# A gated mix of a spectral filter and a Mish MLP: exchange 1 in eight full-width writes and eight half-width reads, a reordered start and a moved end

## The chip, the core and the metric

The kernel runs on one core of one Trainium2 chip. The metric is device microseconds for one execution of the program. A profiled execution also has a span: the time from its first to its last instruction, which is a little shorter than the time. Times inside the span are given in us from its start. The engines are TensorE (PE; its weight loads are PEld), VectorE (DVE), ScalarE (ACT), GpSimd (POOL) and SyncE (SP). SP, ACT and POOL each issue transfers into a queue of their own; the 16 DMA engines serve all queues.

## The reference

Input `x` is 2048 rows of 512 in bfloat16. Two branches are computed and mixed row by row:

```
g = sigmoid(sum(x * gate_w))                       # one number per row
a = irfft2( rfft2(x) * (w_r + i w_i) )             # 2-D FFT over rows and columns, filter, back
h = x @ w1 + b1 ;  b = (h * tanh(softplus(h))) @ w2    # 512 -> 1792 -> 512, Mish
out = g * a + (1 - g) * b
```

Both branches use the same `x` (`A_x`); the second input of that shape (`B_x`) is not read.

## The kernel before, in words

All of the arithmetic that counts is matmul. The MLP is cut into 4 chunks of 512 rows. `mm1` (line 855) makes one of 14 column groups of a chunk from four matmuls of 128x512; ACT applies Mish (line 862). `mm2` (line 879) makes a tile of 128 output rows from 14 matmuls. The FFT is written as small matmuls against tables of cosines: `tr` transposes `x` (534), `a1` transforms along columns (572), `s1` (603) and `s2` (744) are the two factors of the transform along rows, the filter is multiplied in on DVE (`wm`) and combined on POOL (`wz`), `s2i` (775), `s1i` (804) and `a1i` (816) go back. `s2c` (699) is a small side calculation on the same input as `s2`. `s1` uses 64 rows of the array at a time, `s2` and `s2c` squares of 64x32, `s2i` 32x64; the other matmuls use all 128 rows.

Between `s1` and `s2`, and between `s2i` and `s1i`, the data must change partitions. That is done through DRAM: **exchange 1** writes `Y1` (in `Ybuf`) to the scratch tensor `scr1` (lines 613-615) and reads it back into `In2` (in `Abuf`, lines 682-685); **exchange 2** does the same with `scr2` (786, 791). Exchange 1 needs all of its eight groups of rows written before the first read. A group is two `s1` results: DVE or ACT copies them from PSUM to `Ybuf` (`e2`, line 610), and two transfers per group, one for each `rho` (even and odd partitions), write 64 partitions each. Four reads of 128 partitions follow. `s2` of step 0 needs read 0 alone; `s2c` needs all four.

The order of the work on each engine is not written by hand. Every operation is a task with an assumed duration and a priority, and a list scheduler (`_Graph.schedule`, 203-317) walks through them with assumed times at which loads land (`LAND`), a time up to which PE is counted at half speed (`COLD`), and a small random part in the priorities (`SEED`, `NOISE`). It fixes each engine's order when the program is built; at run time engines wait on semaphores, and each engine executes strictly in that order. Loads of `x`, `w1` and tables are issued at the start by SP and ACT in turns, `w2` and the filter weights `WT` by POOL.

At the start PE runs 16 matmuls on a zeroed tile that nobody reads (`warm`, 482-485); DVE sets that tile to zero first (477). At the end SP, having issued its last store, waits for every load that it has not yet waited for (940-943), and then for all stores (944). The last output tile is computed in two halves of 256 columns (`part`, 870-895), each with its own matmuls, its own DVE operation (891) and its own store.

Of the kernel before, what the change touches and what calls it, by code (L numbers as in the profile page):

```python
# [13 lines left out]
NT = 16  # L14
# [12 lines left out]
def _build_consts():  # L27
# [30 lines left out]
    def ee(g, rho, u):  # L58
        return 16 * g + 8 * rho + u

    a = np.arange(64)
    e_q = np.array([ee(g, rho, u) for u in range(8) for g in range(4) for rho in range(2)])
# [39 lines left out]


def _kind(name):
    return name.split("_")[0] if "_" in name else name.rstrip("0123456789")
# [47 lines left out]
class _Graph:  # L153
# [49 lines left out]
    def schedule(self):  # L203
# [13 lines left out]
        rng = np.random.RandomState(SEED)  # L217
        prio = {id(t): t.prio + OFFS.get(_kind(t.name), 0.0) + NOISE * rng.uniform(-1, 1) for t in tasks}
# [8 lines left out]
        while left:  # L227
# [92 lines left out]
NBF = 14  # L320
# [5 lines left out]
SEED = 1294  # L326
NOISE = 0.02
OFFS = {}
# [3 lines left out]
NWARM = 16  # L332
COLD = 4.5
LAND = dict(ld_x0=2.8, ld_x1=3.0, ld_x2=3.5, ld_x3=3.7, ld_w1_0_0=5.6, ld_w1_0_1=5.2,
            ld_fd=5.8, ld_b1=4.7, ld_w1_2_0=7.6, ld_w1_2_1=7.2, ld_x4=9.1, ld_x6=8.4,
            ld_w1_4_0=10.6, ld_w1_4_1=9.9, ld_x8=11.9, ld_m10=13.2, ld_x12=14.5, ld_w1_8_0=15.2,
            ld_w1_8_1=15.9, ld_m11=17.3, ld_w1_12_0=17.7, ld_w1_12_1=18.1, ld_gw=18.4, ld_sm=20.1,
            ld_gd=20.3)
# [3 lines left out]
def _build(nc, A_x, A_w_r, A_w_i, B_x, B_w1, B_b1, B_w2, gate_w, out):  # L342
# [3 lines left out]
    scr1 = nc.dram_tensor("scr1", (2, 32, 64, 256), BF)  # L346
# [4 lines left out]
    with es:  # L351
# [64 lines left out]
        scr1_w = scr1.rearrange("rho b q k -> rho q b k")  # L416
        scr1_r = scr1.rearrange("rho b (ri j) k -> (rho b ri) (j k)", ri=2)
# [52 lines left out]
        t_id = G.add("ident", "pool", 0.3, lambda e: e.affine_select(out=ident[:, :], in_=ident[:, :], pattern=[[1, 2], [2, 64]],  # L470
# [6 lines left out]
        G.add("wz", "dve", 0.3, lambda e: e.memset(act[:, 2, 0, :], 0.0), writes=["warm"])  # L477
        G.add("ebz", "pool", 0.2, lambda e: e.memset(b1f[:, 0:1], 0.0), writes=["b1z"])
        t_tab = G.add("table", "act", 1.3, lambda e: e.activation(b1f[:, 1:2], b1f[:, 0:1], AF.Mish), reads=["b1z"], writes=["b1t"], prio=0.0)

        pw = _Ps([6])
        tw = []
        for i in range(NWARM):
            tw.append(pe(f"warm{i}", mm(256), lambda e: e.matmul(ps[:, pw.bank, 0:256], act[:, 2, 0, 0:128], act[:, 2, 0, 0:256], start=True, stop=True),  # L484
                         reads=["warm"], alloc=pw if i == 0 else None, frees=[pw], prio=0.0, deps=tw[-1:]))
# [15 lines left out]
        ld_w1(0, 2, both)  # L501
        dma("ld_fd", FDs[:].rearrange("p r k -> p (r k)"), d_FD[:], writes=["FD"], nbytes=131072)
        dma("ld_b1", braw[:, :], B_b1.rearrange("(ft p) -> ft p", p=128), writes=["braw"], nbytes=3584, queue="pool", deps=[t_id])
# [23 lines left out]
        for t0, w in ((0, 1), (1, 1), (2, 2), (4, 2), (6, 2), (8, 2), (10, 2), (12, 2), (14, 2)):  # L527
            pt = _Ps(SPEC[::-1])
            def f_tr(e, t0=t0, w=w, pt=pt):
                ins = None  # L530
                for i in range(w):
                    for c in range(4):
                        o, d0 = (c * w + i) * 128, 256 * (c // 2) + c % 2
                        ins = e.transpose(psb[:, pt.bank, o:o + 128], xo[:, t0 + i, d0:d0 + 255:2], ident[:, :])  # L534
                return ins

            pe(f"tr{t0}", 4 * w * mm(128), f_tr, reads=[("x", t0 + i) for i in range(w)] + ["ident"], writes=[("ptr", t0)], alloc=pt)
            evict(f"evx{t0}", 512 * w, lambda t0=t0, w=w: xT[:, :, 128 * t0:128 * (t0 + w)],
                  lambda pt=pt, w=w: psb[:, pt.bank, 0:512 * w].rearrange("p (c j) -> p c j", c=4), rate=2.0,
                  reads=[("ptr", t0)], writes=[("xT", t0 + i) for i in range(w)], frees=[pt], engs=("dve",))  # L540
            if t0 == 2:
                pb = _Ps(SPEC[::-1])
                pe("tr_small", 0.1, lambda e, pb=pb: e.transpose(psb[:, pb.bank, 0:14].rearrange("p (a b) -> p a b", b=2), braw[0:14, :],
                                                                    ident[0:14, :].rearrange("p (b a) -> p a b", b=2)[:, 0:7, :]),
                   reads=["braw", "ident"], writes=["ptb"], alloc=pb)
                G.add("ev_small", "dve", 0.2, lambda e, pb=pb: e.tensor_copy(out=b1f[:, :], in_=psb[:, pb.bank, 0:14]),
                      reads=["ptb", "b1t"], writes=["b1f"], frees=[pb])
# [3 lines left out]
        for t in range(NT):  # L551
# [39 lines left out]
            if t % 4 == 3:  # L591
# [17 lines left out]
                for tp, p1 in zip((t - 3, t - 1), p1s):  # L609
                    evict(f"e2_{tp}", 1024, lambda tp=tp: Y1[:, 2 * tp:2 * tp + 4, :].rearrange("p (i b) k -> p i b k", b=2),  # L610
                          lambda p1=p1: ps[:, p1.sl, :].rearrange("p b (i k) -> p i b k", i=2),
                          reads=[("p1", tp)], writes=[("Y1", tp)], frees=[p1], prio=PR["sp"] + E2P, engs=("act",) if tp % 4 else ("dve",))
                    for rho in range(2):
                        dma(f"r1w{tp}{'ab'[rho]}", scr1_w[rho][:, 2 * tp:2 * tp + 4, :], Y1[rho::2, 2 * tp:2 * tp + 4, :], reads=[("Y1", tp)],
                            writes=[("scr1", tp, rho)], nbytes=64 * 4 * 512, prio=PR["sp"] + 1.0, tail=0.5, bw=300e3)
        S1R = [("scr1", i, rho) for i in range(0, NT, 2) for rho in range(2)]
# [64 lines left out]

        for v in range(4):
            dma(f"r1r{v}", In2[:, 2 * v:2 * v + 2].rearrange("p u g k -> p (u g k)"),
                scr1_r[:, 2048 * v:2048 * v + 2048], reads=S1R, writes=[("In2", rho, 2 * v + i) for i in range(2) for rho in range(2)], deps=s1_tasks,
                nbytes=128 * 4096, prio=PR["sp"] + 1.0)
        r1rs = [dma_ for dma_ in G.tasks[-4:]]
# [154 lines left out]
        def store(t):  # L841
            dma(f"out{t}", ov[:, t - 1:t + 1, :], xo[:, t - 1:t + 1, :], reads=[("o", t - 1), ("o", t)],
                nbytes=128 * 2048, is_out=True, prio=PR["fin"], tail=0.6)

        mm2s = {}
        for c in range(NCH):
            hb = c % 3
            G.cur_prio = PR["mm1"] - c
            for ft in range(NFT):
                pd = _Ps(DENSE[c])  # L850

                def f_mm1(e, c=c, ft=ft, pd=pd):
                    ins = None
                    for i in range(4):
# [10 lines left out]
                      reads=[("pm", c, ft), "b1f"], writes=[("act", hb, ft)] + (["warm"] if hb == 2 and ft == 0 else []), frees=[pd], prio=PR["mish"])  # L865
            G.cur_prio = PR["mm2"] - c
            for tl in range(4):
                t = 4 * c + tl

                for part in range(2):  # L870
                    if part == 0 or t == NT - 1:
                        pd = _Ps(DENSE2[c])
                    cs_ = slice(256 * part, 256 * part + 256) if t == NT - 1 else slice(0, 512)
# [9 lines left out]
                    tk = pe(f"mm2_{t}_{part}", 7 * mm(512), f_mm2,  # L883
# [4 lines left out]
                    if t < NBF or (t < NT - 1 and part == 0):  # L888
                        continue
                    G.add(f"fin_{t}_{part}", "dve", dve_dur(256 if t == NT - 1 else 512, True),  # L890
# [4 lines left out]
                        nbytes=65536 * (1 if t == NT - 1 else 2), is_out=True, prio=PR["fin"], tail=0.6)  # L895
# [22 lines left out]
        def run_engine(ename, eobj):  # L918
            seen = {}
            for t in order[ename]:  # L920
                need = {}
# [18 lines left out]
            if ename == "sp":  # L940
                for t in G.tasks:
                    if t.isdma and t.sem is not out_sem and seen.get(t.sem.num, 0) < t.semval:
                        eobj.wait_ge(t.sem, t.semval)
# [67 lines left out]
```

## Time and profile before

| | |
|---|---|
| median of 3 runs | 133.02 us (132.97 to 135.15) |
| the profiled execution | 132.8 us, its span 131.1 us |
| PE busy | 124.9 us, 95% of the span |
| DVE, ACT, POOL busy | 89.3, 72.2, 58.3 us |
| mean granted TensorE clock | 1.00 |
| moved by DMA | 21.09 MB, mean 161 GB/s |
| first `mm1` starts / last matmul ends | 7.29 / 128.15 us |

How to read it: PE is busy almost throughout, so what matters is when its useful work starts, whether a wait opens a hole in it, and what comes after its last matmul. PE's share of the span says nothing of the first and the last: idle matmuls count as busy, and a matmul on a small part of the array counts like any other.

### The profile page before, as it was taken

To read this page: it belongs to the slowest core of one execution; us is meant where nothing else is said; L and a number is where in the kernel's file an instruction comes from. 1 tells how busy PE (TensorE), PEld (TensorE's weight loads), DVE (VectorE), ACT (ScalarE), POOL (GpSimd) and SP (SyncE) were. 2 spreads that over 40 slices of the span, in tenths; PEclk is the share of its full clock that TensorE was granted. 3 is DMA by queue.
4 is the path that set the end of the run, shared out by engine and by line. 5 is a ranking of instruction groups with operands and counts; after the bars stand their busy time and mean duration, and the time that the engine had idled before them with its cause. 6 is when DMAs were issued, how large, how long until landed. Compare 5 with 4: busy or idle time off the path is not lost.

```text
span 131.1 us, 2497 instructions
## 1 busy us (share of the span) xinstructions
PE 124.9 (95%) x930; PEld 64.9 (50%) x947; DVE 89.3 (68%) x159; ACT 72.2 (55%) x119; POOL 58.3 (44%) x89
## 2 busy tenths in 40 slices
PE   6979999999999999999999999999999999999991
PEld 4646666544454444344343333344566555555580
DVE  0437989979797941296498994500267996899691
ACT  0437557898878787621236867922347741562420
POOL 6000009700020774059479979100019676879710
PEclk9999999999999999999999999999999999999999
DMA  3899964999956544956104050466910042022213
GB/s 106 258 293 420 386 209 81 368 287 228 223 138 199 171 123 109 336 235 250 75 26 134 3 160 5 143 177 171 404 70 0 0 156 84 5 80 83 80 46 116
DMA packets 16892, 21.09 MB, mean 161 GB/s; under 512 B 1200, under 2 KB 13360, under 8 KB 16496
## 3 DMA queue, kind: packets, MB, share of 16 engines
q1 hardware_dynamic: 14736, 15.95, 36.4%
q0 software_dynamic: 896, 3.94, 11.8%
q10 hardware_dynamic: 1248, 1.05, 2.6%
q8 instruction: 7, 0.11, 0.4%
q14 instruction: 5, 0.04, 0.1%
HBM read 14.64 MB, written 6.29 MB: 160 GB/s over the span
## 4 chain that ended last, share of the span: by engine, by line
PE 94%; issue 2%; DVE 1%; ACT 1%
PE ps L855 37%; PE ps L879 37%; PE ps L534 4%; PE ps L603 3%; PE ps L804 3%; PE ps L572 3%; PE ps L816 3%; PE ps L484 2%; PE ps L744 2%; PE ps L775 1%; ACT act L862 1%; DVE Tg L464 1%; DVE xo L891 0%; DVE act L477 0%; PE ps L699 0%
## 5 line engine op out<-in xcount | busy, mean ns | idle before, releaser
L855 PE MATMUL ps<-xT,w_sb 128*128 128x512 bf16 x214 | 51.0, 380 | 1.6 <-DVE Tg L464 0.8
L879 PE MATMUL ps<-w_sb,act 128*128 128x512 bf16 (+1 forms) x231 | 50.4, 366 | 0.4
L862 ACT ACTIVATE act<-ps,b1f 128x512 bf16<-128x512 f32 x56 | 38.5, 687 | 14.9 <-PE ps L855 14.1
L879 PEld LDWEIGHTS ps<-w_sb,act 128*128 128x128 bf16 x238 | 22.4, 98 | 22.1 <-issue 0.6
L855 PEld LDWEIGHTS ps<-xT,w_sb 128*128 128x128 bf16 x224 | 20.0, 98 | 25.5 <-ACT act L862 2.5
L464 POOL TENSOR_TENSOR Tg<-Qb 128x256 bf16<-128x256 f32 x29 | 21.6, 772 | 20.8 <-DVE Qb L827 20.8
L837 ACT ACTIVATE xo<-ps,omg 128x512 bf16<-128x512 f32 x14 | 9.6, 687 | 25.7 <-PE ps L879 22.9
L464 POOL TENSOR_TENSOR Zb<-Qb 128x510 bf16<-128x510 f32 x16 | 19.9, 1269 | 8.3 <-DVE Qb L464 8.3
L464 DVE TENSOR_TENSOR Qb<-ps,WT 128x1024 f32<-128x1024 f32 x16 | 18.8, 1218 | 6.3 <-PE ps L744 5.5
L827 DVE SCALAR_TENSOR_TENSOR Qb<-ps,gcol,Qb 128x256 f32<-128x256 f32 x32 | 13.6, 474 | 2.5 <-PE ps L816 2.5
L459 DVE CAST Ybuf<-ps 128x1024 bf16<-128x1024 f32 x8 | 9.8, 1220 | 4.6 <-PE ps L775 2.9
L464 DVE TENSOR_TENSOR Abuf<-ps,Tg 128x512 bf16<-128x512 f32 x16 | 10.3, 684 | 3.6 <-ACT Tg L579 3.6
L459 DVE CAST Zb<-ps 128x512 bf16<-128x512 f32 x7 | 4.7, 688 | 11.6 <-PE ps L804 11.2
L621 DVE SCALAR_TENSOR_TENSOR Tg<-xo,Tg 128x512 bf16<-128x512 bf16 x16 | 11.0, 686 | 0.3
L821 ACT ACTIVATE Qb<-ps,gcol 128x256 f32<-128x256 f32 x16 | 7.2, 470 | 7.0 <-PE ps L816 7.0
L429 POOL DMA_DIRECT2D w_sb<-in_B_w_dram x2 | 1.9, 974 | 16.9 <-DMA sm<-c_sm 16.9
L464 DVE TENSOR_TENSOR xo<-xo,Tg 128x512 bf16<-128x512 bf16 x14 | 9.3, 690 | 0.2 <-ACT xo L837 0.2
L460 ACT ACTIVATE Ybuf<-ps 128x1024 bf16<-128x1024 f32 x8 | 8.2, 1023 | 1.5 <-PE ps L603 1.2
L459 DVE COPY xT<-ps 128x1024 bf16<-128x1024 bf16 (+1 forms) x9 | 5.4, 627 | 4.6 <-PE ps L534 4.4
L640 POOL COPY wrv<-WT 128x2 bf16<-128x2 bf16 x2 | 0.4, 187 | 12.8 <-DMA WT<-in_A_w_i_dram 12.8
L804 PE MATMUL ps<-m1g,Abuf 128*128 128x128 bf16 x64 | 5.7, 219 | 0.0
L816 PE MATMUL ps<-GDs,Zb 128*128 128x128 bf16 x64 | 5.7, 219 | 0.0
(69 smaller groups left out, 88.4 us busy)
## 6 DMA issues: line engine op xcount, KB each, us to landing
Abuf<-scr SPq DMA_DIRECT2D x8, 512.0 KB, 5.4
scr<-Ybuf SPq DMA_DIRECT2D x16, 128.0 KB, 2.2
scr<-Ybuf SPq DMA_DIRECT2D x4, 512.0 KB, 3.2
w_sb<-in_B_w_dram POOLq DMA_DIRECT2D x2, 896.0 KB, 6.9
out_dram<-xo SPq DMA_DIRECT2D x7, 256.0 KB, 2.0
WT<-in_A_w_r_dram POOLq DMA_DIRECT2D x4, 257.0 KB, 9.1
WT<-in_A_w_i_dram POOLq DMA_DIRECT2D x4, 257.0 KB, 12.8
xo<-in_A_x_dram SPq DMA_DIRECT2D x2, 512.0 KB, 8.0
```

Source lines behind the costliest of these rows:

```text
L459: fs = {"dve": ("dve", dve_dur(n, rate=rate), lambda e: e.tensor_copy(out=dst(), in_=src())), "act": ("act", act_dur(n), lambda e: e.activ ...
L460: "act": ("act", act_dur(n), lambda e: e.activation(dst(), src(), AF.Copy))}
L464: f = lambda e: e.tensor_tensor(out=o(), in0=i0(), in1=i1(), op=op)
L621: lambda e, t=t: e.scalar_tensor_tensor(out=junk, in0=xo[:, t, :], scalar=1.0, in1=gwb, op0=ALU.mult, op1=ALU.mult, accum_out=gdot[:, t:t ...
L804: ins = e.matmul(ps[:, p4.bank, o:o + 128], T2r[:, 2 * t + bx, par::2], G1s[:, 16 * bx + t, :], start=True, stop=True)
L816: ins = e.matmul(ps[:, p5.bank, 128 * i:128 * i + 128], TT[:, sl, 2 * par + ri, :], GDs[:, i, :], start=True, stop=True)
L821: lambda e, t=t, sl=sl, p5=p5: e.activation(gC[:, sl, :].rearrange("p (i n) -> p i n", i=2), ps[:, p5.bank, :].rearrange("p (i n) -> p i n ...
L827: lambda e, t=t, sl=sl, p5=p5, o=o, op=op: e.scalar_tensor_tensor(out=st1[:, sl, o::2, :], in0=ps[:, p5.bank, :].rearrange("p (i n) -> p i ...
L837: G.add_multi(f"bev_{t}", [("act", act_dur(512, True), lambda e: e.activation(xo[:, t, :], ps[:, pd.bank, :], AF.Copy, scale=omg[:, t:t + ...
L855: ins = e.matmul(ps[:, pd.bank, :], w1_sb[:, i, 128 * ft:128 * (ft + 1)], xT[:, i, 512 * c:512 * c + 512], start=(i == 0), stop=(i == 3))
L862: lambda e, ft=ft, pd=pd, hb=hb: e.activation(act[:, hb, ft, :].rearrange("p (t a b) -> p t a b", t=4, b=2), ps[:, pd.bank, :].rearrange(" ...
L879: ins = e.matmul(ps[:, pd.bank, cs_], act[:, hb, ft, 128 * tl:128 * (tl + 1)], w2_sb[:, ft, cs_], start=(ft == 0), stop=(ft == NFT - 1))
```

## The change

- **Exchange 1.** The columns of the `s1` table are put in another order (`e_q`), so that the two `rho` halves of a result are partitions in blocks rather than alternating ones. The scratch tensor becomes (32, 128, 256). A group is written by one transfer of 128 partitions: 8 writes instead of 16. A step of `In2` is read by two transfers, one for each `rho`, of 64 partitions each (0-63 and 64-127): 8 reads instead of 4. The bytes are the same.
- **Start.** The idle matmuls read a constant of ones that the program's preamble already holds, so the DVE memset is gone; there are 18 of them (14 ahead of the transposes) instead of 16 (11 ahead). The transpose of row tiles 2 and 3 and its copy are split in two. The load of `b1` moves from POOL's queue to ACT's, between two `w1` loads, and its transpose stands behind the first `mm1` group rather than ahead of it. POOL builds the identity matrix after the flip matrix.
- **End.** SP's waits for all loads move from the end of the program to a place ahead of its first store. The last tile is cut into 384 and 128 columns. The store of the last pair of earlier tiles and the store of the 384 columns move from SP's queue to ACT's.
- **Order.** The random part of the priorities is drawn otherwise and with other seeds, so the scheduler puts many operations in another order. Row tiles 6, 7 are transposed ahead of 4, 5. On PE ten `mm1` groups and seven `mm2` matmuls stand between the last `s1` and the first `s2` (eleven `mm1` groups before), then the 16 `s2` matmuls and 14 `mm2` matmuls (21 before) ahead of `s2c`. One more `s2` group stands alone: the short groups of matmuls on a part of the array (`s1`, `s2`, `s2c`, `s2i`) come in 14 runs instead of 13. On POOL, a small copy that waits for the first `s2i` now stands behind two `wz` of the next step.

```diff
-    e_q = np.array([ee(g, rho, u) for u in range(8) for g in range(4) for rho in range(2)])
+    e_q = np.array([ee(g, rho, u) for rho in range(2) for u in range(8) for g in range(4)])
...
-        rng = np.random.RandomState(SEED)
-        prio = {id(t): t.prio + OFFS.get(_kind(t.name), 0.0) + NOISE * rng.uniform(-1, 1) for t in tasks}
+        noise = np.random.RandomState(SEED).uniform(-1, 1, len(tasks))
+        for m in MORE:
+            rng = np.random.RandomState(m)
+            pick = rng.uniform(size=len(tasks)) < 0.02
+            noise[pick] = rng.uniform(-2, 2, len(tasks))[pick]
+        prio = {id(t): t.prio + NOISE * x for t, x in zip(tasks, noise)}
...
-NWARM = 16
-COLD = 4.5
+NWARM = 18
+COLD = 3.9
...
-    scr1 = nc.dram_tensor("scr1", (2, 32, 64, 256), BF)
+    scr1 = nc.dram_tensor("scr1", (32, 128, 256), BF)
...
-        scr1_w = scr1.rearrange("rho b q k -> rho q b k")
-        scr1_r = scr1.rearrange("rho b (ri j) k -> (rho b ri) (j k)", ri=2)
+        scr1_w = scr1.rearrange("b m k -> m b k")
+        scr1_r = scr1.rearrange("b (ri rho j) k -> rho (b ri) (j k)", ri=2, rho=2)
...
-        G.add("wz", "dve", 0.3, lambda e: e.memset(act[:, 2, 0, :], 0.0), writes=["warm"])
...
+        one_w, one_m = (nc.const_aps.tensor(1.0, (128, n), BF) for n in (128, 256))
...
-            tw.append(pe(f"warm{i}", mm(256), lambda e: e.matmul(ps[:, pw.bank, 0:256], act[:, 2, 0, 0:128], act[:, 2, 0, 0:256], start=True, stop=True),
+            tw.append(pe(f"warm{i}", mm(256), lambda e: e.matmul(ps[:, pw.bank, 0:256], one_w, one_m, start=True, stop=True),
...
         ld_w1(0, 2, both)
+        dma("ld_b1", braw[:, :], B_b1.rearrange("(ft p) -> ft p", p=128), writes=["braw"], nbytes=3584, queue="act")
         dma("ld_fd", FDs[:].rearrange("p r k -> p (r k)"), d_FD[:], writes=["FD"], nbytes=131072)
-        dma("ld_b1", braw[:, :], B_b1.rearrange("(ft p) -> ft p", p=128), writes=["braw"], nbytes=3584, queue="pool", deps=[t_id])
...
-        for t0, w in ((0, 1), (1, 1), (2, 2), (4, 2), (6, 2), (8, 2), (10, 2), (12, 2), (14, 2)):
+        for t0, w in ((0, 1), (1, 1), (2, 1), (3, 1), (4, 2), (6, 2), (8, 2), (10, 2), (12, 2), (14, 2)):
...
-                    for rho in range(2):
-                        dma(f"r1w{tp}{'ab'[rho]}", scr1_w[rho][:, 2 * tp:2 * tp + 4, :], Y1[rho::2, 2 * tp:2 * tp + 4, :], reads=[("Y1", tp)],
-                            writes=[("scr1", tp, rho)], nbytes=64 * 4 * 512, prio=PR["sp"] + 1.0, tail=0.5, bw=300e3)
+                    dma(f"r1w{tp}", scr1_w[:, 2 * tp:2 * tp + 4, :], Y1[:, 2 * tp:2 * tp + 4, :], reads=[("Y1", tp)],
+                        writes=[("scr1", tp)], nbytes=128 * 4 * 512, prio=PR["sp"] + 1.0, tail=0.7, bw=290e3, issue=0.4)
...
         for v in range(4):
-            dma(f"r1r{v}", In2[:, 2 * v:2 * v + 2].rearrange("p u g k -> p (u g k)"),
-                scr1_r[:, 2048 * v:2048 * v + 2048], reads=S1R, writes=[("In2", rho, 2 * v + i) for i in range(2) for rho in range(2)], deps=s1_tasks,
-                nbytes=128 * 4096, prio=PR["sp"] + 1.0)
+            for rho in range(2):
+                r = slice(64 * rho, 64 * rho + 64)
+                r1rs.append(dma(f"r1r{v}{'ab'[rho]}", In2[r, 2 * v:2 * v + 2].rearrange("p u g k -> p (u g k)"),
+                                scr1_r[rho][:, 2048 * v:2048 * v + 2048], reads=S1R, writes=[("In2", rho, 2 * v + i) for i in range(2)], deps=s1_tasks,
+                                nbytes=64 * 4096, prio=PR["sp"] + 1.0, issue=0.42, tail=1.7))
...
             dma(f"out{t}", ov[:, t - 1:t + 1, :], xo[:, t - 1:t + 1, :], reads=[("o", t - 1), ("o", t)],
-                nbytes=128 * 2048, is_out=True, prio=PR["fin"], tail=0.6)
+                nbytes=128 * 2048, is_out=True, prio=PR["fin"], tail=0.6, queue="act" if t == NBF - 1 else "sp")
...
-                    cs_ = slice(256 * part, 256 * part + 256) if t == NT - 1 else slice(0, 512)
+                    cs_ = slice(384 * part, 384 + 128 * part) if t == NT - 1 else slice(0, 512)
...
+                if ename == "sp" and t.isdma and t.sem is out_sem and not seen.get("loads"):
+                    seen["loads"] = 1
+                    for l in G.tasks:
+                        if l.isdma and l.sem is not out_sem and seen.get(l.sem.num, 0) < l.semval:
+                            seen[l.sem.num] = l.semval
+                            eobj.wait_ge(l.sem, l.semval)
...
-                for t in G.tasks:
-                    if t.isdma and t.sem is not out_sem and seen.get(t.sem.num, 0) < t.semval:
-                        eobj.wait_ge(t.sem, t.semval)
```

## The prediction

> **What bounds the kernel.** I first cut the span where the useful matmuls begin and end (busy time in three stretches: span so far, then PE, PEld, DVE, ACT, POOL).
>
> ```profile
> 0.00:7.29 7.29, 5.22 (x34) 3.58 (x35) 2.64 (x7) 1.49 (x2) 2.04 (x11) 1.00 0.65 190
> 7.29:128.15 120.86, 119.64 (x897) 61.33 (x914) 86.15 (x152) 70.74 (x117) 56.22 (x78) 1.00 0.51 161
> 128.15:131.10 2.95, 0.00 (x0) 0.00 (x0) 0.48 (x1) 0.00 (x0) 0.00 (x0) 1.00 0.28 85
> ```
>
> In the middle PE is busy for 119.64 of 120.86 us, and part of the rest is matmul records that the trace lacks. So no wait in the middle can be shortened to any profit: the time is a start of 7.29, PE's work of 120.86 and an end of 2.95. A change there can only lose, by opening a hole, or alter the work. The start, from the timeline of PE, and of the transfers issued between 1.6 and 2.4 us:
>
> ```profile
> 3.81 1.92 PE L534 MATMUL ps<-ident,xo 128*128 128x128 bf16 x16
> 5.89 0.61 PE L484 MATMUL ps<-act 128*128 128x256 bf16 x4
> 7.29 1.46 PE L855 MATMUL ps<-xT,w_sb 128*128 128x512 bf16 x6 [0.79 <-DVE Tg L464]
> ```
> ```profile
> w_sb<-in_B_w_dram ACTq DMA_DIRECT2D x2, 128.0 KB, 4.8
> w_sb<-in_B_w_dram SPq DMA_DIRECT2D x1, 128.0 KB, 5.5
> ```
>
> The first `mm1` waits for `xT` and two `w1` transfers. The release is put down to a DVE operation that `mm1` doesn't read; the copy that it does read (5.77 + 0.69) was done at 6.46. SP's `w1` transfer, issued at 1.71, landed 5.5 later, at 7.2: that is what it waited for. Exchange 1, on PE:
>
> ```profile
> 43.78 1.06 PE L603 MATMUL ps<-Abuf,m1g 64*128 64x256 bf16 x16
> 44.78 9.67 PE L855 MATMUL ps<-xT,w_sb 128*128 128x512 bf16 x43
> 54.38 0.63 PE L744 MATMUL ps<-Abuf,sm 64*32 64x512 bf16 x16
> 54.94 4.71 PE L879 MATMUL ps<-w_sb,act 128*128 128x512 bf16 x20
> 59.57 0.24 PE L699 MATMUL ps<-Abuf,sm 64*32 64x8 bf16 x16
> ```
>
> No gap: while the data goes through DRAM, PE does `mm1` and `mm2`. The exchange is hidden, with a margin seen below. The end: the DVE rows of the last tile, SP's waits, and the transfer issued after 128.5:
>
> ```profile
> L891 DVE SCALAR_TENSOR_TENSOR xo<-ps,omg,Tg 128x256 bf16<-128x256 f32 x2 | 1.0, 476 | 0.6 <-PE ps L879 0.6
> ...
> L891 DVE SCALAR_TENSOR_TENSOR xo<-ps,omg,Tg 128x512 bf16<-128x512 f32 x1 | 0.7, 737 | 0.0
> ```
> ```profile
> L943 SPq EVENT_SEMAPHORE  x18: 27/28/28, 129.1 to 130.5; - x18
> ```
> ```profile
> out_dram<-xo SPq DMA_DIRECT2D x1, 64.0 KB, 1.5
> ```
>
> The last store, issued at 128.68, has landed at 130.2, but SP is still walking through its 18 waits, two semaphores each, until 130.6.
>
> **Start: -0.35 (from 0 to -0.5).** Idle matmuls: PE need not wait for the memset (0.91 + 0.27) and can start at about 0.85, since SP and ACT issue from 0.80. Fourteen at 0.213 (half clock, from the 2.53 of eleven) end at 3.83, where `x` lands anyway (0.80 + 3.0). Gain nothing; a clock that opens 0.4 sooner shortens the transposes, but they don't end the wait. `xT`: with the copy split, DVE ends at about 6.2 instead of 6.46; also not the last. What counts is the `w1` transfer at 7.2. Its twin on ACT's queue, of equal size and issue time, took 4.8. In the change ACT issues `b1` first and its next `w1` transfer an issue later (0.4 to 0.6), so SP's gets a larger share. I take the mean of both rows, 5.15: landing at 6.85, first `mm1` at 6.94. Ends: it stays at 7.29; or it starts so early that the next load binds. That is `x` tiles 4 and 5, landed at 10.66 (3.90 + 6.8); in the new order 3.93 of PE work (two `mm1` 1.73, `a1` 0.89, `mm1` 0.86, a transpose set 0.45) stand ahead of them, so a start before 6.8 is lost again: -0.5. `b1` must land before the second `mm1` group, at 7.8; ACT's transfers at that place take 4.8 from 2.4, so 7.2. What else ACT issues an issue later (`w1` 7.7, `x` 6 and 7 8.5, `w1` 10.8) is needed at 9.6, 10.4 and 12.1. The copy of `b1` now stands behind two DVE sums (0.69 each), at 7.6; the first Mish needs it at 8.0. POOL's identity is done by 2.5, needed at 3.8.
>
> **Exchange 1: +0.15 (from 0 to +2.45).** The writes: 16 issues of 0.62 become 8; the 128-partition write of exchange 2 takes 0.36 to issue. After the last `s1` starts (43.85) the last write was issued at +4.0 and landed at +6.2, the reads were issued from +6.5, the last landed at +14.6 (51.71 + 6.8 = 58.5), and `s2c` came at +15.7. New: two issues, at +2.1 and +2.5; landing 2.2 (128 KB) to 3.2 (512 KB) later, so about +5.0; reads from +5.4. This gain of 1.1 buys no time, since PE never waited; it buys margin, and the new order spends some: `s2c` comes at 1.03 + 10 x 0.864 + 7 x 0.216 + 0.62 + 14 x 0.216 = +14.85. The reads are the unknown, as no read of 64 partitions is in the trace. Two rows bound them, 32 partitions at the low end (the `WT` loads, 29 to 33) and 128 at the high end (reads 54 to 57.5; last columns: clock, share of DMA time, GB/s):
>
> ```profile
> 29.00:33.00 4.00, 4.00 (x24) 1.92 (x22) 3.78 (x8) 3.54 (x7) 0.00 (x0) 1.00 1.02 228
> ...
> 54.00:57.50 3.50, 3.50 (x31) 1.33 (x29) 2.64 (x3) 1.00 (x2) 0.21 (x1) 1.00 1.00 385
> ```
>
> The DMA engines were full in both, so 32 partitions cost rate. 2.1 MB take 5.4 at 385 and 9.2 at 228. The old reads took 8.1 in all, so 2.7 is latency. Last landing: +13.5 or +17.3; against +14.85, a hole of 0 or 2.45. 64 is one doubling from either, so I take the mean rate, 306: 6.9, landing at +15.0, hole 0.15. Eight issues at 0.43 (3.4) lie under the transfer. Read pair 0 is needed at +11.2 and lands by +10.
>
> The Trainium skill ("SBUF — State Buffer", section "Door 1: The DMA port swizzle") speaks against this: partitions 0-63 reach the same 8 of 16 ports as 0-31, about 218 GB/s, and its next section says that two transfers on the two halves serialize. The `WT` row agrees with it for 32 partitions (228); no row here shows 64. By that rule the hole is that of the low end; it is rival B. By its 218 the reads would take 9.6 and the hole be 2.8, which makes 135.1 (an estimate).
>
> **Order: +0.1.** A run of 16 `s2` takes 0.56 (54.38 to 54.94), one of 8 takes 0.33 (59.64 to 59.97), so a run costs 0.10 whatever its length; there is one more. Matmuls are otherwise the same (14 x 384 + 14 x 128 columns for 28 x 256). DVE's work from 7 to 45 us is reordered too; its waits are covered by `mm1` groups on PE, and I count nothing (rival D has a price for such a loss).
>
> **End: -0.45 (from -0.2 to -0.6).** The 18 waits go ahead of the first store. SP was idle for 14.2 us before that one (104.36); without that cover the first stores would be 1.5 late, with 24 us to spare. At the end the store's landing, not the walk, is then last: -0.35. The last DVE operation has 128 columns: 0.476 less half of the 0.261 that 256 to 512 costs, 0.345: -0.13. The DVE operation on 384 columns (0.61) fits under the last 14 matmuls (0.75), and its store, issued by ACT, lands 1.5 to 1.8 after the issue, before the last one; nothing stands behind it on ACT. The last store moves 256 bytes per partition, which no store here does; from -0.05 to +0.15. Sum about -0.45.
>
> **Sum.** 132.8 (profiled) - 0.35 + 0.15 + 0.1 - 0.45 = 132.25. The median of the runs is 0.2 above the profiled execution: 132.4.
>
> **Rivals.**
> A, the above: PE full from 6.9 on. 132.4, own range 131.8 to 133.0. Chance 0.55.
> B, slower: the 64-partition reads go at the 32-partition rate and `s2c` stops PE. 132.4 - 0.15 + 2.45 = 134.7. For it: the `WT` row, with engines full. Against: that transfer came by POOL's queue, where 128 partitions (`w2`) got 323, not 385; and both halves stand in the queue at once. It eats the gain if the hole is over 0.75, that is, with reads under 280 GB/s. Chance 0.25.
> C, the start doesn't move: `w1` lands at 7.2 whatever stands around it, and 132.75 comes out. For it: its bytes and its place on SP's queue are the same. Chance 0.12.
> D, POOL is late for the last `s2i`: the last `wz` ended at 82.47, that `s2i` started at 83.09, a margin of 0.6. The new order has 27.1 us instead of 28.7 from the first `s2` to there; POOL was busy for 21.7 and idle for 3.4 in between, of it 1.7 in the wait that the moved copy removes. If that wait stays: 132.4 + 1.0 to 1.7, 133.8. Chance 0.08.
>
> Range: 131.7 to 134.6 leaves out some 0.04 below and 0.15 above (B's upper part). Two per cent, about what a measurement of this kernel can tell from no change, is 2.7 us: under 130.4 needs a gain that no row holds (0.01); over 135.7 needs B and another loss (0.04); within, 0.95.
>
> **What would show it.** First `mm1` at 6.8 to 7.0, its last `w1` at 6.85. No wait of PE on `Abuf<-scr` over 0.3 before `s2c`; 2 or more is B. 0.36 per write issue. A span that ends 2.5 after the last matmul, with no waits of SP there. Wrong if: PE has a hole elsewhere, or the 256-byte rows land late.

## The result, and the profile after

The changed kernel takes 134.24 us (median of six runs, 134.02 to 134.77) against 132.99 for the kernel before in the same session (median of six). The ratio is 1.0104, with a 95% interval of 1.0082 to 1.0126: slower by 1.0%, inside the band of 2%, on the other side of no change than the forecast 132.4. The profiled execution took 134.35 with a span of 132.6 (before: 132.8 and 131.1). Medians here and below are of all executions of a kernel, and ratios leave out the slow ones, those more than 1.5% above its fastest (the worst took 396 us in run 8 and 333 in run 11), so the two need not agree to the last digit.

The same three stretches as in the prediction, cut at the first `mm1` and at the end of the last matmul (span so far, then PE, PEld, DVE, ACT, POOL; last: clock, DMA share, GB/s):

```profile
0.00:6.20 6.20, 5.37 (x34) 4.22 (x34) 1.72 (x5) 1.12 (x1) 1.22 (x10) 1.00 0.59 171
6.20:130.34 124.14, 121.88 (x917) 60.72 (x915) 87.79 (x155) 70.88 (x117) 57.15 (x79) 1.00 0.54 160
130.34:132.60 2.26, 0.00 (x0) 0.00 (x0) 0.35 (x1) 0.00 (x0) 0.00 (x0) 1.00 0.20 58
```

The start is shorter by 1.09 (7.29 to 6.20) and the end by 0.69 (2.95 to 2.26), but the middle is longer by 3.28 (120.86 to 124.14): in sum 1.5, which is what the span grew by. The middle now has holes. The largest is at exchange 1, here in PE's timeline of the changed kernel:

```profile
44.63 1.06 PE L603 MATMUL ps<-Abuf,m1g 64*128 64x256 bf16 x16
45.63 8.81 PE L856 MATMUL ps<-xT,w_sb 128*128 128x512 bf16 x40
54.27 1.67 PE L880 MATMUL ps<-w_sb,act 128*128 128x512 bf16 x7
55.87 0.63 PE L745 MATMUL ps<-Abuf,sm 64*32 64x512 bf16 x16
56.43 3.19 PE L880 MATMUL ps<-w_sb,act 128*128 128x512 bf16 x14
61.41 0.24 PE L700 MATMUL ps<-Abuf,sm 64*32 64x8 bf16 x16 [1.78 <-DMA Abuf<-scr]
```

`s2c` (line 700) was due at 59.46, fourteen matmuls of 0.216 after 56.43, and starts at 61.41: 1.95 lost (the view counts 1.78, since a matmul's modelled end comes after its successor could start). Of this, 0.09 stands there in the kernel before too, where 21 matmuls from 54.94 on end at 59.48 and `s2c` starts at 59.57. What it waits for are the reads of exchange 1, whose last landing the trace has at 61.28. How they were issued (SP's timeline), how long they took (the page's DMA issues: KB each, median us to landing) and the rate meanwhile (two stretches):

```profile
50.05 4.97 SPq L429 DMA_DIRECT2D Abuf<-scr  x8
```
```profile
Abuf<-scr SPq DMA_DIRECT2D x8, 256.0 KB, 5.6
```
```profile
54.00:57.00 3.00, 3.00 (x29) 1.13 (x27) 0.64 (x1) 0.98 (x2) 0.00 (x0) 1.00 0.98 236
57.00:60.00 3.00, 2.63 (x13) 0.98 (x10) 3.00 (x4) 0.34 (x1) 0.08 (x1) 1.00 0.98 232
```

The 16 DMA engines are about as full as in the kernel before (0.98 and 1.00), but they move 232 to 236 GB/s, where the old reads moved 385. Eight reads of 256 KB land 1.06 apart, which is 248 by the landings; the old ones, of 512 KB, landed 1.39 apart, 377.

The other losses in the middle are small. In PE's timeline around 18 us, and around 107:

```profile
17.44 0.61 PE L572 MATMUL ps<-FDs,Tg 128*128 128x128 bf16 x8
18.42 1.89 PE L856 MATMUL ps<-xT,w_sb 128*128 128x512 bf16 x8 [0.38 <-issue]
```
```profile
106.67 0.39 PE L805 MATMUL ps<-m1g,Abuf 128*128 128x128 bf16 x4
107.12 0.40 PE L817 MATMUL ps<-GDs,Zb 128*128 128x128 bf16 x4
```

At 18 a step takes 0.54 too long: `mm1` waits for `w1` columns 8 to 11, whose transfers landed at 17.61 and 18.33 (before: 15.98 and 16.67). At 107 four matmuls of 0.056 are followed after 0.45, so 0.23 are lost, to DVE, which does sums ahead of the operation that frees the bank. Further 0.18 lie at 9.0, 0.21 are the little transpose of `b1` that now stands between `mm1` groups, and 0.1 is the one more run of partial-array matmuls. With the 1.86 that is new at `s2c` these make 3.1 of the 3.28.

### The profile page after: what moved, and what is told of

The parts are those of the page before. It is cut to its first block, busy times and chain, and to the rows that moved or that the text cites. A ratio compares the mean times of both kernels' runs of the same rounds, so it can differ in the third digit from the quotient of the medians.

```text
span 132.6 us, 2507 instructions
## 1 busy us (share of the span) xinstructions
PE 127.2 (96%) x949; PEld 64.9 (49%) x949; DVE 89.9 (68%) x160; ACT 72.0 (54%) x117; POOL 58.4 (44%) x89
## 4 chain that ended last, share of the span: by engine, by line
PE 87%; DMA 5%; SPq 3%; DVE 2%; issue 1%
PE ps L856 35%; PE ps L880 32%; DMA Abuf<-scr 5%; PE ps L534 3%; SPq L429 3%; PE ps L603 3%; PE ps L484 3%; PE ps L572 3%; PE ps L817 3%; PE ps L805 2%; PE ps L776 2%; PE ps L745 1%; DVE xo L464 1%; DVE Qb L828 1%; DVE xo L892 0%
## 5 line engine op out<-in xcount | busy, mean ns | idle before, releaser
L856 PE MATMUL ps<-xT,w_sb 128*128 128x512 bf16 x224 | 52.8, 380 | 0.4 <-issue 0.4
L880 PE MATMUL ps<-w_sb,act 128*128 128x512 bf16 (+2 forms) x238 | 51.9, 367 | 0.0
L880 PEld LDWEIGHTS ps<-w_sb,act 128*128 128x128 bf16 x238 | 21.8, 98 | 22.5 <-issue 1.3
L464 POOL TENSOR_TENSOR Tg<-Qb 128x256 bf16<-128x256 f32 x30 | 22.7, 783 | 19.6 <-DVE Qb L828 19.5
L459 DVE CAST Zb<-ps 128x512 bf16<-128x512 f32 x8 | 5.4, 688 | 12.0 <-PE ps L805 11.3
L464 DVE TENSOR_TENSOR xo<-xo,Tg 128x512 bf16<-128x512 bf16 x14 | 8.5, 644 | 0.0
L817 PE MATMUL ps<-GDs,Zb 128*128 128x128 bf16 x64 | 6.2, 219 | 0.1
L464 DVE TENSOR_TENSOR Tg<-xT 128x1024 bf16<-128x1024 bf16 x8 | 5.2, 686 | 1.2 <-PE ps L572 1.1
```

What stands on the lines that cost most here:

```text
L459: fs = {"dve": ("dve", dve_dur(n, rate=rate), lambda e: e.tensor_copy(out=dst(), in_=src())), "act": ("act", act_dur(n), lambda e: e.activ ...
L464: f = lambda e: e.tensor_tensor(out=o(), in0=i0(), in1=i1(), op=op)
L817: ins = e.matmul(ps[:, p5.bank, 128 * i:128 * i + 128], TT[:, sl, 2 * par + ri, :], GDs[:, i, :], start=True, stop=True)
L856: ins = e.matmul(ps[:, pd.bank, :], w1_sb[:, i, 128 * ft:128 * (ft + 1)], xT[:, i, 512 * c:512 * c + 512], start=(i == 0), stop=(i == 3))
L880: ins = e.matmul(ps[:, pd.bank, cs_], act[:, hb, ft, 128 * tl:128 * (tl + 1)], w2_sb[:, ft, cs_], start=(ft == 0), stop=(ft == NFT - 1))
```

## Experiments

The scheduler adds noise to each task's priority from a random series, so one task more or fewer reorders the whole kernel. So in every kernel here the order of instructions, engines and PSUM banks of the kernel that it starts from is written out, and `schedule` only plays it back. The edits then change what they say and nothing else. Ratios are to the kernel before, run on the same chip in the same session, where it took 132.76 to 132.91.

**1. Alternate partitions instead of halves.** Changed kernel, and:

```diff
-    r1rs.append(dma(f"r1r{v}{'ab'[rho]}", In2[r, 2 * v:2 * v + 2]...
+    r1rs.append(dma(f"r1r{v}{'ab'[rho]}", In2[rho::2, 2 * v:2 * v + 2]...
```

> The changed kernel, its order of instructions written out and kept, but each of the eight reads of exchange 1 lands in every second partition (offset rho, step 2) instead of in one half of the partitions. Source, size, number and queue of the reads stay. The spectral data then stand in the wrong partitions, so this run is for its time alone. Halves theory (a read into 64 neighbouring partitions is written at a lower rate, about 250 GB/s here, than one that spreads over all 128): the reads go at about 385 GB/s as in the kernel before, the last lands some 2 us earlier (near 59.2 in place of 61.3), the hole of 1.95 us ahead of s2c is gone, 132.2 to 132.7. Rival, number and layout (eight transfers instead of four, rows now spread over DRAM by rho): nothing changes, hole 1.9, 134.2.

Measured 132.61, ratio 0.9999 (0.9968 to 1.003); so 1.0% less than the changed kernel. The rate in two stretches of the reads:

```profile
53.50:56.50 3.00, 3.00 (x15) 1.22 (x13) 0.00 (x0) 1.99 (x3) 0.00 (x0) 1.00 0.94 275
56.50:59.50 3.00, 2.95 (x28) 1.23 (x28) 2.46 (x3) 0.00 (x0) 0.00 (x0) 1.00 0.82 300
```

Number, size, source and queue are the same, so which partitions a read reaches is worth 236 to some 288 GB/s, and the hole shrinks from 1.95 to 0.50. But 385 is not held: the first two reads landed 0.73 apart, which is 359 GB/s, then the sixteen parts of the third landed over 2.0 us (54.83 to 56.85), and those of every later read over 1.8 to 2.1, where those of the first two took 0.7 to 0.9; the reason is open. So the halves theory holds for most of the hole, and not for the last of it.

**2. Four reads of 128 partitions out of the new layout.**

```diff
-    for rho in range(2):
-        r = slice(64 * rho, 64 * rho + 64)
-        r1rs.append(dma(..., In2[r, 2 * v:2 * v + 2]..., scr1_r[rho][:, 2048 * v:2048 * v + 2048], ...
+    r1rs.append(dma(f"r1r{v}", In2[:, 2 * v:2 * v + 2]..., scr1_r[:, :, 2048 * v:2048 * v + 2048], ...
```

> The changed kernel, its order kept, with its eight writes and its layout of scr1, but the data come back in four reads of 128 partitions (the source pattern has rho as an outer dimension). Halves theory: 385 GB/s, no hole, last landing near 58.5 to 59, 132.2 to 132.6, faster than the kernel before by some 0.5 us, since the gains at the start (0.95) and the end (0.69) then stand against the hole of 0.5 at 18 us alone. Rival, number of transfers: the same time, so this run does not tell it apart (the run with alternate partitions does). Rival, layout in DRAM: the reads still take about 9 us, 134.2. Rival, the reordered instructions and not the exchange: 134.2.

Measured 168.49, ratio 1.2684 (1.2615 to 1.2752). No theory had foreseen it. PE's waits, and the stretch in which the reads run:

```profile
PE ps L698 <- DMA Abuf<-scr: 24.8, 1, 24.8
PE ps L743 <- DMA Abuf<-scr: 7.0, 1, 7.0
```
```profile
56.00:92.00 36.00, 5.34 (x29) 1.78 (x30) 4.61 (x4) 0.69 (x1) 2.48 (x2) 0.65 0.13 52
```

The DMA engines are busy for 0.13 of the time, two of sixteen, and each read counts two landings instead of sixteen. The source's outermost dimension is now rho, of size 2.

**3. The same with the outer dimensions exchanged.**

```diff
-    scr1_r[:, :, 2048 * v:2048 * v + 2048]
+    scr1_r[:, :, 2048 * v:2048 * v + 2048].rearrange("rho q x -> q rho x")
```

> As the run with four reads of 128 partitions out of the new layout, which took 10 us for each read, with the two outer dimensions of the source exchanged: 64 rows of two in place of two rows of 64. Bytes, pieces of 4 KB and their number are the same; the rows land in another order of partitions, so the output is not the reference's and the run is for its time. If the outermost dimension decides over how many DMA engines a read is spread (that run showed two landings for each read, the others sixteen): sixteen landings, about 385 GB/s, no hole at s2c, 132.3 to 132.9. Rival, a pattern of three dimensions out of this layout is slow as such: about 168 again.

Measured 132.47, ratio 0.9965 (0.9949 to 0.998). Sixteen landings for each read, and in the middle of them:

```profile
55.00:58.50 3.50, 3.50 (x31) 1.33 (x30) 0.95 (x1) 1.17 (x2) 0.00 (x0) 1.00 0.98 382
```

So the outermost dimension decided, and neither the layout of `scr1` nor the three dimensions cost anything: 382 GB/s out of the new layout. Such a read needs the partitions in the order (b, ri, rho), which the matmuls of line 745, with rho as halves of the array, do not take. I know of no form of the change that has the reads of this run and the right output.

**4. Exchange 1 undone in the changed kernel; 5. exchange 1 alone in the kernel before.** The edit is the part of the diff on `e_q`, `scr1`, `r1w` and `r1r`, backwards and forwards.

> The changed kernel, its order kept, with exchange 1 undone: sixteen writes of 64 alternate partitions, four reads of 128, the old layout of scr1. Halves theory: reads issued at about +6.5 after the last s1, the last landed at +14.6, s2c due at +14.85: no hole there; 132.3 to 132.9, which is 1.3 to 1.9 below the changed kernel. Since the data then come in time, POOL may be late for the last s2i (its margin was 0.6, and about 0.7 of its chain moves with PE): 0 to 0.6 of that is in the range. Rival, the reordered instructions cost the time whatever the exchange: 134.0 to 134.4.

> The kernel before, its order kept, with exchange 1 of the change alone: eight writes of 128 partitions, eight reads of 64, the new layout of scr1. Halves theory: reads issued about 1.1 earlier after the last s1, at +5.4, the last lands at about +16.6 as in the changed kernel; s2c is due at +15.7, so a hole of 0.9 (0.6 to 1.2) opens ahead of it: 133.9 against 133.0. Rival, the reordering of the changed kernel makes its hole and the exchange is harmless: 133.0, no wait at s2c.

Undone: 132.71, ratio 0.9993 (0.9974 to 1.0012). Alone: 134.1, ratio 1.0092 (1.0061 to 1.0122). `s2c` in PE's timeline, first of the run with the exchange undone, then of the run with it alone:

```profile
56.30 3.19 PE L879 MATMUL ps<-w_sb,act 128*128 128x512 bf16 x13
59.42 0.24 PE L699 MATMUL ps<-Abuf,sm 64*32 64x8 bf16 x16
59.77 0.41 PE L744 MATMUL ps<-Abuf,sm 64*32 64x512 bf16 x8
```
```profile
54.91 4.71 PE L880 MATMUL ps<-w_sb,act 128*128 128x512 bf16 x20
60.98 0.24 PE L700 MATMUL ps<-Abuf,sm 64*32 64x8 bf16 x16 [1.36 <-DMA Abuf<-scr]
```

The exchange by itself costs 0.9% in the old order, and taking it out of the new order gives 1.1% back. So it is the whole of the slowdown; all else in the change together comes to no measurable difference. The hole of the second run was 1.53, more than the 0.6 to 1.2 expected: its reads took 11.5 from first issue to last landing, not 11.2, and `s2c` was due at 59.45. With the exchange undone, `s2c` is on time, but the `s2` behind it then waits for DVE (59.42 to 59.77; 0.28 of it is wait), which the larger hole had covered. That takes back 0.28 of the 1.95: 1.7 us are regained in the profiled span (132.6 to 130.9), 1.5 in the medians.

**6. The two halves on two queues.**

```diff
+    queue=("sp", "pool")[rho]
```

> The changed kernel, its order kept, but the four reads into partitions 64 to 127 are issued by POOL, behind gpow (which ends at 52.1), instead of by SP, so that reads into both halves are under way at once. If the two halves are limited each by its own way into SBUF and one queue merely hands them over one after the other: from about 54.5 on both run together near 385 GB/s, last landing near 58.5, hole 0 to 0.3, 132.3 to 132.7. If the transfers into halves are slow whatever stands beside them (the DMA engines are occupied for longer by each packet): 250 GB/s, last landing 61 to 61.5, hole 1.7 to 2.1, 134.0 to 134.4.

> The changed kernel with the reads into partitions 64 to 127 on POOL's queue, this time ahead of gpow, so that the reads into both halves are issued side by side from about 50 on (in the first trial of this POOL issued only when most of the other half had landed, which tested little). If the two halves have each their own limit and can be filled at once: near 385 GB/s in all, the last landing near 58, no hole, 132.3 to 132.9. If the DMA engines are held longer by each packet into a half, whatever the other queue does: 250 GB/s, the last landing 60.5 to 61.5, a hole of 1.2 to 2.0, 133.5 to 134.4.

The first trial settled little: POOL issued only from 53.59, 2.0 behind SP, and two of the other half's four reads had landed (55.44 and 56.67) well before the first of its own did (60.07); it took 136.48, ratio 1.0244 (1.0179 to 1.031), and its `s2` already had to wait 2.7 for that read. In the second, reads were issued by SP at 49.86 to 51.68 and by POOL at 50.35 to 51.97: 133.7, ratio 1.008 (1.0053 to 1.0108). Rate and hole:

```profile
54.00:57.00 3.00, 2.76 (x28) 0.96 (x25) 1.13 (x4) 0.80 (x2) 1.47 (x1) 1.00 1.05 244
57.00:60.00 3.00, 2.70 (x12) 1.08 (x11) 3.00 (x4) 0.21 (x1) 0.00 (x0) 1.00 0.86 240
```
```profile
56.56 3.19 PE L880 MATMUL ps<-w_sb,act 128*128 128x512 bf16 x13
60.70 0.24 PE L700 MATMUL ps<-Abuf,sm 64*32 64x8 bf16 x16 [0.95 <-DMA Abuf<-scr]
```

Two queues side by side move 240 to 244 GB/s, hardly more than one (232 to 236). What is gained against the changed kernel is that the issues overlap and the last read lands at 60.57, 0.7 sooner.

**7. `s2c` later on PE.** Changed kernel; in the written order `s2c` goes behind the `s2` of pair 1 and seven more `mm2` matmuls.

> The changed kernel with one thing moved: s2c stands behind the second s2 of pair 1 and seven more mm2 matmuls on PE, so that it is due 1.8 later, at about 61.3, when the last read lands. If PE's wait there is all that costs: the hole is gone, 132.3. But what comes after s2c stays where it was in time, while PE arrives 1.95 earlier: z0 was ready 1.1 before the first s2i and POOL's last product 0.6 before the last s2i, and about 0.7 of POOL's chain can move up. So I expect 0.6 to 1.3 of the gain, 132.9 to 133.6, with new waits of PE on POOL ahead of s2i. Rival, the hole just moves with the reads: 134.2.

Measured 132.74, ratio 0.9997 (0.9982 to 1.0012): all of the gain, not the half that I expected.

```profile
60.30 0.41 PE L745 MATMUL ps<-Abuf,sm 64*32 64x512 bf16 x8 [0.36 <-DVE Qb L464]
60.64 1.68 PE L880 MATMUL ps<-w_sb,act 128*128 128x512 bf16 x7
62.26 0.24 PE L700 MATMUL ps<-Abuf,sm 64*32 64x8 bf16 x16
...
64.23 3.18 PE L880 MATMUL ps<-w_sb,act 128*128 128x512 bf16 x14
67.34 0.64 PE L776 MATMUL ps<-Zb,sm 32*64 32x512 bf16 x16
```

The only wait of PE left in this stretch is the 0.36 on DVE, and the first `s2i` (line 776) starts without one. So the slow reads cost nothing in themselves; they cost because one reader of all eight stood too early on PE.

**8. The end: closing waits back behind the stores (with exchange 1 undone); 9. the end alone on the kernel before.**

```diff
-    if ename == "sp" and t.isdma and t.sem is out_sem and not seen.get("loads"): ...
+    (the loop over the loads' semaphores behind the last store, as before)
```

> The run with exchange 1 undone, and SP's closing waits put back behind the last store. If the walk through the waits is what ends the kernel when it stands last: from the last matmul to the end 2.6 to 2.75 in place of 2.26, the time 0.35 to 0.5 longer than with exchange 1 undone alone. Rival, the last store's landing ends the kernel in both: no difference.

> The kernel before, its order kept, with the end of the change alone: SP's closing waits ahead of the first store, the last tile as 384 and 128 columns, two of the last stores on ACT's queue. If the walk through the waits and the last DVE operation end the kernel before: 2.3 from the last matmul to the end in place of 2.95, 0.5 to 0.7 faster, 132.1 to 132.4 against 132.8. Rival, the last store (256 bytes per partition) lands later and takes it back: 132.7 to 132.9.

With the waits last: 133.61, ratio 1.005 (1.0018 to 1.0082), 0.6% above the run without this edit. SP's waits in it, by line (duration min/median/max, first and last start):

```profile
L943 SPq EVENT_SEMAPHORE  x18: 27/28/28, 130.1 to 131.6; - x18
```

They end 0.5 before the span does (132.1), and from the start of the last matmul to the end of the span it takes 3.05 in place of 2.49. The end alone on the kernel before: 132.37, ratio 0.9959 (0.994 to 0.9978), 0.5 faster as expected. Its end:

```profile
128.41:130.70 2.29, 0.01 (x1) 0.00 (x0) 0.35 (x1) 0.00 (x0) 0.00 (x0) 1.00 0.37 113
```

**10. The start.** On top of the end alone: idle matmuls on the constant and `b1` by ACT (first run); the same with 14 in place of 11 idle matmuls ahead of the transposes (second run); that without moving `b1` (third run).

```diff
+    dma("ld_b1", ..., queue="act")
     dma("ld_fd", ...)
-    dma("ld_b1", ..., queue="pool", deps=[t_id])
```

> The kernel before with the end of the change (132.37 in its own run) and now two parts of its start as well: b1 issued by ACT between its two w1 transfers instead of by POOL, and idle matmuls on a constant, so that the DVE memset and PE's wait for it go. The split of the third transpose set is left out. The prediction's term: the first mm1 earlier by 0.35, and the time with it: 132.0. Next load theory (the loads take a fixed time in all, and PE that starts earlier waits for the w1 columns behind, which b1 pushes back by one issue on ACT): the first mm1 between 6.2 and 7.0, a hole of 0.3 to 1.4 within the next 6 us, the sum of both within 0.3 of the 7.2 to 7.5 that start and holes come to with the old start, and the time 132.2 to 132.7.

> The run with the end and two parts of the start on the order of the kernel before, with three more idle matmuls ahead of the transposes (14, as the changed kernel has). With 11 of them the idle run ended 0.6 before the first transpose, and PE's matmuls took twice their time until 9.4, which no other run shows: that cost some 1.7 and spoilt the test of the start. If that gap was the cause: full speed from about 4.5 as in the changed kernel. Then, the prediction's term: first mm1 and time 0.35 earlier than with the end alone (132.37, ratio 0.996): 132.0, ratio 0.993. Next load theory: first mm1 at 6.2 to 7.0, a hole of 0.3 to 1.4 in the next 6 us, time 132.2 to 132.6.

> As the run before it, but b1 stays on POOL's queue as in the kernel before: of the start only the idle matmuls on a constant, 14 of them ahead of the transposes. If b1's place is what lets w1 land earlier: w1 of SP's queue lands near 7.2 again and the first mm1 comes at 7.0 to 7.4. If it is scatter of the loads: first mm1 6.3 to 7.3, as likely early as with b1 moved, and a time within 0.3 of that run.

The first run: 133.09, scattered from 131.59 to 133.84 (ratio 0.9976, 0.9943 to 1.0008); its profile is of one of the longer executions, 133.59. PE's timeline in it, and in the second run:

```profile
0.83 2.51 PE L484 MATMUL ps<-const-bfloat16-1.0 128*128 128x256 bf16 x11 [0.83 <-PEq L999]
3.73 2.06 PE L534 MATMUL ps<-ident,xo 128*128 128x128 bf16 x16 [0.39 <-DMA xo<-in_A_x_dram]
...
6.88 3.25 PE L855 MATMUL ps<-xT,w_sb 128*128 128x512 bf16 x8
```
```profile
0.83 3.15 PE L484 MATMUL ps<-const-bfloat16-1.0 128*128 128x256 bf16 x14 [0.83 <-PEq L999]
3.77 1.99 PE L534 MATMUL ps<-ident,xo 128*128 128x128 bf16 x16
...
6.61 1.89 PE L855 MATMUL ps<-xT,w_sb 128*128 128x512 bf16 x8
8.33 1.06 PE L572 MATMUL ps<-FDs,Tg 128*128 128x128 bf16 x16
10.19 0.81 PE L855 MATMUL ps<-xT,w_sb 128*128 128x512 bf16 x3 [0.80 <-DMA w_sb<-in_B_w_dram]
```

Eight `mm1` matmuls take 3.25 in the one and 1.89 in the other: in the first run six of them came 0.427 apart in place of 0.216, so PE ran at half speed until 9.4. The second run has full speed by 6.2, ahead of `mm1`: 132.36 (131.58 to 133.72), ratio 0.9957 (0.9929 to 0.9985). The third, `b1` on POOL: 132.22 (131.90 to 132.75), ratio 0.9947 (0.9927 to 0.9968), the lowest ratio of all. Neither differs measurably from the end alone (0.9959). How long the second and third run's transfers of SP's `w1` took from issue to landing, first the one issued at 1.7, then the one at 3.3 (a fence for each run):

```profile
w_sb<-in_B_w_dram SPq DMA_DIRECT2D x1, 128.0 KB, 4.5
...
w_sb<-in_B_w_dram SPq DMA_DIRECT2D x1, 128.0 KB, 6.6
```
```profile
w_sb<-in_B_w_dram SPq DMA_DIRECT2D x1, 128.0 KB, 5.2
...
w_sb<-in_B_w_dram SPq DMA_DIRECT2D x1, 128.0 KB, 6.2
```

In the changed kernel they are 4.4 and 5.9, in the kernel before 5.5 and 5.5. In these four a sooner first landing goes with a later second one, but that is no more than a tendency: in run 2 the two took 4.9 and 4.8, in run 7 5.2 and 6.8. Over the profiles (us; holes are PE's losses from the first `mm1` to 22, without the 0.21 of `b1`'s transpose; left out are the first run here, with its half speed, and the first trial of run 6, with 6.76 and 2.1):

| `b1` issued by | profiles | first `mm1` | holes | sum |
|---|---|---|---|---|
| POOL | 4 | 6.95 (6.61 to 7.29) | 0.34 (0 to 0.60) | 7.29 (7.2 to 7.5) |
| ACT | 10 | 6.52 (6.20 to 6.96) | 0.90 (0 to 1.59) | 7.42 (6.7 to 8.2) |

The order of the operations differs between the two rows as well, so they do not show what `b1`'s place does by itself; what they show is that an earlier first `mm1` was on average paid back by 22 us.

**11. The small waits of the new order taken out**, with exchange 1 undone.

> The changed kernel with exchange 1 undone, and two small waits of PE that its profile still shows taken out by order alone: the two s2 of pair 1 stand together behind the seven mm2 matmuls that follow s2c (PE waited 0.28 for DVE there, and one run of partial-array matmuls less saves 0.1), and one sum of DVE stands behind the two STT that release a bank (PE waited 0.23 there). If each was on PE's path: 132.71 less 0.6, 132.0 to 132.3, the fastest of all. Rival, what comes after has no slack, and the waits come back ahead of s2i: 132.5 to 132.8.

Measured 132.31, ratio 0.9968 (0.9948 to 0.9988). PE around `s2c`:

```profile
56.05 3.19 PE L879 MATMUL ps<-w_sb,act 128*128 128x512 bf16 x14
59.18 0.24 PE L699 MATMUL ps<-Abuf,sm 64*32 64x8 bf16 x16
59.35 1.68 PE L879 MATMUL ps<-w_sb,act 128*128 128x512 bf16 x7
60.96 0.63 PE L744 MATMUL ps<-Abuf,sm 64*32 64x512 bf16 x16
```

The wait on DVE is gone and did not come back, though of the 0.6 expected only 0.4 shows between the medians and 0.3 between the ratios, and the intervals of this run and run 4 overlap. This kernel, the end alone, and the end with 14 idle matmuls all beat both the kernel before (by 0.3 to 0.5%) and the changed one (by 1.4 to 1.6%).

## Why the prediction was wrong

- **What bounds the kernel**: right, and the part that carried most. PE full in the middle means that a change there can only lose; it did, by 3.28.
- **Exchange 1, +0.15**: this step failed, and it set the wrong sign. Its frame held: reads issued at +5.42 after the last `s1` starts (foreseen +5.4), `s2c` due at +14.83 (+14.85), issues hidden under the transfer (though the eight took 4.97, not 3.4). The step that failed reads "64 is one doubling from either, so I take the mean rate, 306". The reads went at 232 to 236, nearly the 228 of the 32-partition row, and the last landed at +16.65, not +15.0: hole 1.95, not 0.15. Between ends far apart the middle is no estimate, and the sign hung on it: the text itself had the hole decide from 0.75 on, with reads under 280. Its rival B, with 0.25 the one that happened, had 2.45; what it had too much is mostly latency: 2.7, taken from reads of 512 KB, where the new reads took 11.23 in all, 2.3 more than 2.1 MB take at 234.
- **The rule cited against the change** (the Trainium skill, "SBUF — State Buffer", section "Door 1: The DMA port swizzle") was right for this case, as far as a rate can show it: a transfer into partitions 0 to 63 reaches half of the ports. The Trainium skill (same page, section "Can I just issue two DMAs to hit both halves?") puts two concurrent transfers, one into each half, at 6% over a single one, which on its 218 GB/s is 231 (an estimate); the trace shows 232 to 236 from one queue and 240 to 244 from two. The 9.6 that the prediction made of its 218 was near the 8.9 to 9.0 that the rates of one queue make.
- **Start, -0.35**: in the profile it was -1.09, with 0.72 of holes and 0.21 of the transpose of `b1` behind it, so -0.16 by 22 us. And that is one draw: over the profiles start and holes come to 7.42 with `b1` on ACT and 7.29 with `b1` on POOL, and the times of run 10 show no gain. The step that failed is "What counts is the `w1` transfer at 7.2", which took the landings as fixed numbers. This one landed between 5.8 and 7.2 from one execution to the next, and PE, when early, waited for the loads behind it. The 4.8 of its "twin" was a misreading too: the row is the median of two transfers, and the one issued at 1.73 took 4.3. Rival C's price (nothing comes of the start) came true by luck: it had `w1` stay at 7.2, and here it landed at 6.09.
- **Order, +0.1**: too small. The 0.23 at 107 and the 0.28 of DVE at `s2` (hidden in the changed kernel, seen in run 4) were not priced. The text's "I count nothing" was said of DVE's work from 7 to 45 us, where no loss to DVE over 0.1 shows; both losses lie behind it, where the text did not look.
- **End, -0.45**: -0.69 in the profile, and 0.5 of time in run 9. The mechanism was right; of its two terms the closing waits were worth more than the 0.35 taken (0.56 in run 8).
- **Rival D** (POOL late for the last `s2i`): no run shows it, not even run 7, where PE came 1.95 earlier.
- **The sum**: of the 1.5 by which the profile is longer, 1.86 come from exchange 1, 0.33 from order (0.23 and 0.1), less 0.69 at the end and 0.16 at the start; that makes 1.34, and some 0.2 is not accounted for.

## What to carry over

When the sign of a forecast hangs on one rate that no row shows, price the ends and give the chance to each; do not take the middle. Before a transfer is cut in halves by partition, look at which partitions each half reaches and at the outermost dimension of its source, and measure the rate alone; where a cut must stay, move the one reader that needs all parts behind other work, which here gave back all of it. A first matmul that starts earlier is worth something only if the loads behind it come earlier too; here nothing of it was left by 22 us.

## What the runs showed of the chip

- A read whose source has an outermost dimension of 2 ran on 2 of 16 DMA engines, at 52 GB/s; with 64 outermost the same bytes went at 382. The Trainium skill ("DMA: Bandwidth & Descriptors", section "Rules for kernel authors") states this rule, that the slowest dimension sets the number of engines; the trace agrees, with two landings for each read.
- Reads of 256 KB into 64 alternate partitions went at 275 to 300 GB/s: faster than into a half (236), slower than 512 KB into all 128 (382). What the rest is due to is open; size alone is unlikely, since the first two of them landed 0.73 apart (359 GB/s), and from the third on some parts of each read came late.
- PE's full speed opened at 5.9 in the changed kernel (its idle matmuls come 0.213 apart up to there, the next two 0.16 and 0.14, and the `mm1` behind them 0.216), between 5.6 and 6.2 in the second run of 10, at 3.8 in run 3, the earliest, and at 9.4 in the first run of 10, in which 0.6 of idleness stood ahead of the transposes; there the first eight `mm1` took 1.36 longer. The expectation of the second run has 4.5 for the changed kernel; no matmul of its profile runs at full speed before 5.9. That the gap was the cause is likely and not shown: it is one execution, and filling the gap narrowed the scatter of the times hardly at all. The granted clock in the profile's rows reads 1.00 throughout; only the spacing of the matmuls shows it. The Trainium skill ("TensorE: Matmul & The Clock Gate", section "What's actually happening") describes a free-running window of 3.4 us that must be busy; 9.4 is one such window behind 6.0, near where the second run opened, which agrees; where the windows began no run here shows.
